# Storing a kernel's result in two DMAs, one batch row each, from two issuers

## The chip, the cores and the metric

The kernel runs on one core of one Trainium2 chip. The metric is device time in microseconds (us). The probes below were run once each, and the record marks their state unknown, so they are compared by their traces and not by their times. One run of each kernel was profiled, and its trace gives starts and durations to the nanosecond.

## The reference

One decode step (one token) for a batch of two: an adaptive layer norm, attention over the last 1024 positions of a cache with 32 heads, a second adaptive layer norm and a gated feed-forward layer.

```python
def reference(A_x, A_k_cache, A_v_cache, A_wq, A_wo, B_x, B_w_gate, B_w_up, B_w_down, c, w_mod):
    ...                                   # mod = silu(c) @ w_mod gives sa, ca, ga, sb, cb, gb
    h = _layernorm(x, axis=-1) * (1 + ca) + sa
    x = x + ga * _A_ref(h, A_k_cache, A_v_cache, A_wq, A_wo)
    h = _layernorm(x, axis=-1) * (1 + cb) + sb
    x = x + gb * _B_ref(h, B_w_gate, B_w_up, B_w_down)
    return x                              # (2, 1, 640) bfloat16: 2.5 KB
```

## The kernel before

The kernel streams caches and weights and computes as they come. Only its end matters here. The result stands in `finb`, 128 partitions by 160 columns. Eight of the rows are real: partition 32*i + 16*b holds columns 160*i to 160*i+159 of batch row b (i from 0 to 3, b 0 or 1). One DMA, issued by SyncE, stores all eight rows of 320 bytes, and SyncE waits for it as its last act. `S.dma` records a DMA with the semaphore that it is told to raise by 16; `S.op` records an operation of an engine; both work out the waits from the names read and written.

```python
        def k_dma(dst, src):                                   # L266: the line of every DMA
            return lambda e: e.dma_start(dst, src)
        ...
        S.op("dve", lambda e: e.tensor_tensor(out=fin[:, :], in0=ps[:, BK_OT, CY:CY + DR], in1=modR[:, 5, :], op=ALU.mult),
             reads=[bank(BK_OT), ("modR", 1)], writes=["fin"], name="gb_y")                   # L689
        S.op("dve", lambda e: e.tensor_tensor(out=finb[:, :], in0=fin[:, :], in1=X[:, :], op=ALU.add),
             reads=["fin", "X"], writes=["finb"], name="outR")                                # L691
        S.dma("sp", k_dma(out[:, 0, :].rearrange("b (i n) -> i b n", i=NR), finb[0:P:RB, :]),  # RB = 16
              sem_out, reads=["finb"], name="st_out")

        S.resolve()
        S.emit("sp", nc.sync, tail=lambda e: e.wait_ge(sem_out, 16))                          # L697
```

Of the kernel before, what the change touches and what calls it, by code (L numbers as in the profile page):

```python
# [119 lines left out]
def bass_adaLN_cond__sliding_block_cached__geglu_ffn__decode_kernel(  # L120
# [14 lines left out]
    P = 128  # L135
    B, _, D = A_x.shape
# [6 lines left out]
    NR = 4  # L143
# [31 lines left out]
    RB = 16  # L175
# [11 lines left out]
    with es:  # L187
        S = _Sched(nc, es)
# [54 lines left out]
        finb = sb("finb", [P, DR], BF16)  # L243
# [9 lines left out]
        def bank(k):  # L253
            return ("bank", k)
# [5 lines left out]
        sem_wu = [S.sem("d_wu%d" % i) for i in range(len(WU_SPLIT))]  # L260
        sem_wd = [S.sem("d_wd%d" % i) for i in range(len(WD_SPLIT))]
        sem_ring = [S.sem("d_ring%d" % i) for i in range(NS)]
        sem_out = S.sem("d_out")

        def k_dma(dst, src):
            return lambda e: e.dma_start(dst, src)  # L266
# [57 lines left out]
        for nm, t in (("scT", scT), ("oT", oT), ("aT", aT)):  # L324
# [6 lines left out]
             reads=["ones_f"], writes=["ident_f"], name="ident_f")  # L331
        S.op("pool", lambda e: e.tensor_copy(out=ident_b[:, :], in_=ident_f[:, :]),
             reads=["ident_f"], writes=["ident_b"], name="ident_b")
# [3 lines left out]
             reads=["ones_b"], writes=["selrow"], name="selrow")  # L337
# [3 lines left out]
             reads=["ones_b"], writes=["selg"], name="selg")  # L341
        for b in range(B):
# [4 lines left out]
                 reads=["ones_b"], writes=[("selq", b)], name="selq%d" % b)  # L347
# [4 lines left out]
             reads=["ones_b"], writes=["ztmp"], name="ztmp")  # L352
# [6 lines left out]
             reads=["ones_f", "bcL"], writes=["bcL"], name="bcLh")  # L359
# [5 lines left out]
             reads=["bcR"], writes=["bcR"] + [("bcR", z) for z in range(2)], name="bcRd")  # L365
# [4 lines left out]
             reads=["ident_f"], writes=["mask_h"], name="mask_h")  # L370
        S.op("dve", lambda e: e.tensor_reduce(out=st32[:, :], in_=ident_f[:, :].rearrange("p (i m) -> p m i", m=32), axis=AX.X, op=ALU.add),
             reads=["ident_f"], writes=["st32"], name="st32")
# [3 lines left out]
             reads=["st32"], writes=["selstat"], name="selstat")  # L376
# [3 lines left out]
        def c_T(e):  # L380
            last = None
            for j in range(KT):
# [4 lines left out]
             reads=[bank(BK_T)], writes=["scT"], name="silu")  # L387
        S.op("dve", lambda e: e.tensor_copy(out=X[:, :], in_=xr[:, :]),
             reads=["xr"], writes=["X"], name="x_f32")
# [20 lines left out]
        def ln_mod(tag, opc_idx, s_idx, dst_bf):  # L410
# [7 lines left out]
            def f(e):  # L418
# [14 lines left out]
             reads=["mask_h"], writes=["maskc"], name="maskc")  # L433
        S.op("dve", lambda e: e.tensor_reduce(out=zsel[:, :, X0:X0 + P].rearrange("p q (h m) -> p q h m", m=32)[:, :, :, 0],
                                              in_=ztmp[:, :, :, :].rearrange("p i q h -> p q h i"), axis=AX.X, op=ALU.max),
             reads=["ztmp", "zsel"], writes=["zsel"], name="zsel")

        mod_pe = []
        for half in range(2):
            def f(e, half=half):  # L440
                last = None
                for k in range(KT):
# [9 lines left out]
                 reads=[bank(half)], writes=[("modR", half)], name="mod%d_evac" % half)  # L452
            S.op("dve", lambda e, half=half: e.tensor_scalar(out=opc[:, half, :], in0=modR[:, 3 * half + 1, :], scalar1=1.0, scalar2=None, op0=ALU.add),
                 reads=[("modR", half)], writes=[("opc", half)], name="opc%d" % half)
# [17 lines left out]
        for n in range(NQB):  # L472
            if n % 2 == 0:
                S.op("act", lambda e, n=n: e.activation(out=qrow[:, n * QW:(n + 1) * QW], in_=ps[:, n, :], func=ACTF.Copy),  # L474
                     reads=[bank(n)], writes=[("qrow", n)], name="q1_evac%d" % n)
            else:
                S.op("dve", lambda e, n=n: e.tensor_copy(out=qrow[:, n * QW:(n + 1) * QW], in_=ps[:, n, :]),  # L477
                     reads=[bank(n)], writes=[("qrow", n)], name="q1_evac%d" % n)
        for u, (n, b) in enumerate((n, b) for n in range(NQB) for b in range(B)):
            bk = BK_T + u % 4  # L480
            S.op("pe", lambda e, n=n, b=b, bk=bk: e.matmul(ps[:, bk, :], lhsT=selq[:, b, :], rhs=qrow[:, n * QW:(n + 1) * QW], start=True, stop=True),
                 reads=[("selq", b), ("qrow", n)], writes=[bank(bk)], name="q2_%d_%d" % (n, b))
            S.op("act", lambda e, n=n, b=b, bk=bk: e.activation(out=qbc[:, b, n * QW:(n + 1) * QW], in_=ps[:, bk, :], func=ACTF.Copy),  # L483
                 reads=[bank(bk)], writes=[("qbc", b, n)], name="q2_evac%d_%d" % (n, b))
# [98 lines left out]
        for g in range(NG + 2):  # L583
# [23 lines left out]
            if prev:  # L607
# [5 lines left out]
             reads=[bank(BK_OT)], writes=["oT"], name="oT")  # L613
# [22 lines left out]
        for ci, (r0, nr) in enumerate(WD_SPLIT):  # L636
# [5 lines left out]
             reads=[bank(BK_M), ("modR", 0)], writes=["lnt"], name="ga_attn")  # L642
        S.op("dve", lambda e: e.tensor_tensor(out=X[:, :], in0=lnt[:, :], in1=X[:, :], op=ALU.add),
             reads=["lnt", "X"], writes=["X"], name="x1")
# [3 lines left out]
        def ffn_gu(bk, wv, name, splits):  # L648
            for ci, (k0, nk, key) in enumerate(splits):
# [12 lines left out]
             reads=[bank(0)], writes=["gl"], name="gelu")  # L662
        ffn_gu(1, wu_v, "up", [(k0, nk, ("wu", ci)) for ci, (k0, nk) in enumerate(WU_SPLIT)])
        S.op("dve", lambda e: e.tensor_tensor(out=aR[:, :], in0=ps[:, 1, 0:FT], in1=gl[:, :], op=ALU.mult),
             reads=[bank(1), "gl"], writes=["aR"], name="geglu")

        def a_T(e):
            last = None
            for i in range(NR):
# [7 lines left out]
             reads=[bank(2)], writes=["aT"], name="aT")  # L677
        for ci, (r0, nr) in enumerate(WD_SPLIT):
            def f(e, r0=r0, nr=nr):
# [10 lines left out]
             reads=[bank(BK_OT), ("modR", 1)], writes=["fin"], name="gb_y")  # L690
        S.op("dve", lambda e: e.tensor_tensor(out=finb[:, :], in0=fin[:, :], in1=X[:, :], op=ALU.add),  # L691
             reads=["fin", "X"], writes=["finb"], name="outR")
        S.dma("sp", k_dma(out[:, 0, :].rearrange("b (i n) -> i b n", i=NR), finb[0:P:RB, :]),
              sem_out, reads=["finb"], name="st_out")

        S.resolve()
        S.emit("sp", nc.sync, tail=lambda e: e.wait_ge(sem_out, 16))  # L697
        S.emit("pool", nc.gpsimd)
        S.emit("act", nc.scalar)
        S.emit("dve", nc.vector)  # L700
# [29 lines left out]
```

## Time and profile before

| | before |
|---|---|
| time, median of the three runs before the prediction | 188.83 us (188.71 to 189.14) |
| span of the profiled run | 187.6 us |
| read from HBM | 76.88 MB, 410 GB/s over the span |
| last VectorE operation (`outR`) starts | 185.52 us |
| store: issue starts, lasts | 185.87 us, 0.69 us |
| SyncE's wait for the store after that | 1.0 us |

The page of the kernel before tells what bounds it. In the DMA row each digit is the busy share of the DMA engines in one fortieth of the span, in tenths.

```profile
DMA  7999998999999999999999999999999999999991
...
HBM read 76.88 MB, written 0.00 MB: 410 GB/s over the span
## 4 chain that ended last, share of the span: by engine, by line
DMA 71%; DVE 15%; PE 7%; ACT 2%; SPq 2%; issue 1%
```

The DMA row stands at 9 in 37 of the 40 slices, and DMA is 71% of the chain of waits. The end of that chain, in order of time (start, duration, what), shows where the stream stops and the tail begins:

```profile
152.72 31.64 DMA r<-in_B_w_down_dram
184.37 0.04 issue
184.41 0.72 PE ps L684 x16
185.13 0.02 issue
185.16 0.34 DVE fin L689
185.49 0.02 issue
185.52 0.32 DVE finb L691
```

From 184.37 us on, each step waits for the one before it (it starts at most 0.04 us after that one's end), and nothing else runs. The chain stops at the last compute instruction. The timeline of the same kernel (start, duration, engine, line, operation) has the store. SPq and ACTq stand for the instruction queues of SyncE and ScalarE; the duration of a DMA on them is that of its issue, not of the transfer.

```profile
185.52 0.32 DVE L691 TENSOR_TENSOR finb<-fin,X 128x160 bf16<-128x160 f32 x1
185.87 0.69 SPq L266 DMA_DIRECT2D out_dram<-finb  x1
```

The landing is not a line of the timeline. SyncE's own waits (total us, times, longest us) show it, as the wait of line 697:

```profile
SPq L697 <- DMA out_dram<-finb: 1.0, 1, 1.0
```

So the store takes 0.69 us to issue and a further 1.0 us to land, all on the critical path. The table by stretches shows when its data moves. Its columns are the stretch, its length, busy time by engine, granted clock, DMA share and GB/s.

```profile
185.87:187.15 1.28, 0.00 (x0) 0.00 (x0) 0.00 (x0) 0.00 (x0) 0.00 (x0) 0.50 0.00 0
187.15:187.35 0.20, 0.00 (x0) 0.00 (x0) 0.00 (x0) 0.00 (x0) 0.00 (x0) 0.50 0.07 13
187.35:187.60 0.25, 0.00 (x0) 0.00 (x0) 0.00 (x0) 0.00 (x0) 0.00 (x0) 0.50 0.00 0
```

For 1.28 us after the issue's start no packet moves at all; then all of them go within 0.2 us; then comes about a quarter of a microsecond of waiting until the store has landed.

### The profile page before, as it was taken

The page shows a single profiled execution, that of the slowest core. Times are in us where ns is not written, and L with a number is a line of the kernel's source. Part 1 is how long each engine was busy: PE and PEld are TensorE (multiplying, and loading weights), DVE is VectorE, ACT ScalarE, POOL GpSimd, SP SyncE. Part 2 cuts the span into 40 slices and gives each one's busy share as a digit, 9 for nine tenths or more (in the row PEclk, how much of TensorE's full clock was granted, in tenths as well). Part 3 has the DMA queues.
Part 4 walks back from the last instruction along what each step waited for, and adds up shares of the span by engine and source line. Part 5 has one row for each costly group of instructions (what it writes and reads, how often), then busy time and mean ns, then how long its engine had stood idle before and what let it go on. Part 6 is the DMA issues. An engine that isn't in the chain of part 4 may idle for free.

```text
span 187.6 us, 2409 instructions
## 1 busy us (share of the span) xinstructions
PE 107.5 (57%) x1039; PEld 51.1 (27%) x1039; DVE 98.2 (52%) x147; ACT 29.9 (16%) x72; POOL 5.1 (3%) x23
## 2 busy tenths in 40 slices
PE   0014730742968887676676655675497395364462
PEld 0011200210323443333423323233253152353121
DVE  6131100019588988886595695775865933003211
ACT  3041100082001221112011110210120103103400
POOL 8200000000000000000000000000000000000000
PEclk9999999997587999999879999999969967569696
DMA  7999998999999999999999999999999999999991
GB/s 254 402 451 435 430 459 372 422 435 424 430 422 422 427 425 426 427 424 420 419 432 432 422 423 422 421 438 422 424 423 422 419 488 428 416 384 442 398 396 45
DMA packets 6518, 77.03 MB, mean 411 GB/s; under 512 B 746, under 2 KB 876, under 8 KB 1516
## 3 DMA queue, kind: packets, MB, share of 16 engines
q1 hardware_dynamic: 6492, 76.88, 97.1%
q8 instruction: 8, 0.13, 0.3%
q10 hardware_dynamic: 16, 0.01, 0.0%
q14 instruction: 2, 0.02, 0.0%
HBM read 76.88 MB, written 0.00 MB: 410 GB/s over the span
## 4 chain that ended last, share of the span: by engine, by line
DMA 71%; DVE 15%; PE 7%; ACT 2%; SPq 2%; issue 1%
DMA ring<-in_A_k_cache_dram 37%; DMA ring<-in_A_wq_dram 17%; DMA r<-in_B_w_down_dram 17%; DVE prod L490 9%; PE ps L502 4%; DVE S_sb L509 4%; PE ps L467 2%; SPq L266 2%; ACT qbc L483 2%; DVE ps L485 1%; DVE M L512 1%; ACT qrow L474 1%; PE ps L526 0%; DVE bcR L519 0%; PE ps L684 0%
## 5 line engine op out<-in xcount | busy, mean ns | idle before, releaser
L490 DVE TENSOR_TENSOR prod<-ring,qbc 128x3072 bf16<-128x3072 bf16 x32 | 55.9, 1751 | 14.3 <-DMA ring<-in_A_k_cache_dram 14.3
L502 PE MATMUL ps<-prod,ident_b 128*128 128x512 bf16 x192 | 52.9, 419 | 14.4 <-DVE prod L490 14.4
L502 PEld LDWEIGHTS ps<-prod,ident_b 128*128 128x128 bf16 x192 | 17.5, 104 | 40.2 <-DVE prod L490 17.5
L509 DVE TENSOR_REDUCE S_sb<-ps 128x32 f32<-128x1024 f32 x16 | 19.3, 1206 | 2.1 <-PE ps L502 2.1
L526 PE MATMUL ps<-bcR,bcL 5*128 5x4 f32 x32 | 6.1, 258 | 21.9 <-DVE bcR L519 21.9
L563 ACT ACTIVATE On<-ps,rden 128x384 bf16<-128x384 f32 x16 | 9.3, 580 | 43.5 <-DVE rden L561 21.1
L551 PE MATMUL ps<-ring,E_sb 128*8 128x384 bf16 x256 | 15.5, 369 | 0.0
L534 ACT ACTIVATE E_sb<-Sb_sb 128x128 bf16<-128x128 f32 x16 | 5.0, 310 | 56.4 <-DVE Sb_sb L531 56.4
L467 PE MATMUL ps<-ring,hT 128*2 128x512 bf16 x60 | 6.7, 626 | 9.8 <-DMA ring<-in_A_wq_dram 8.8
L526 PEld LDWEIGHTS ps<-bcR,bcL 5*128 5x128 f32 x32 | 4.7, 183 | 26.1 <-DVE bcR L519 26.1
L477 DVE CAST qrow<-ps 128x512 bf16<-128x512 f32 x1 | 0.7, 692 | 15.7 <-PE ps L467 15.7
L622 PE MATMUL ps<-ring,oT 128*17 128x160 bf16 x192 | 5.5, 294 | 5.6 <-DMA ring<-in_A_wo_dram 5.6
L531 DVE TENSOR_TENSOR Sb_sb<-S_sb,ps 128x128 f32<-128x128 f32 x16 | 4.6, 287 | 7.6 <-PE ps L526 7.6
L540 PEld LDWEIGHTS ps<-denp,maskc 128*128 128x128 f32 x32 | 7.1, 224 | 3.7 <-ACT E_sb L534 0.9
L641 DVE TENSOR_TENSOR lnt<-ps,modR 128x160 f32<-128x160 f32 x1 | 0.3, 325 | 12.6 <-PE ps L622 12.6
L445 PE MATMUL ps<-r,scT 128*17 128x480 bf16 x40 | 4.3, 597 | 3.9 <-DMA r<-in_w_mod_dram 3.9
L622 PEld LDWEIGHTS ps<-ring,oT 128*17 128x17 bf16 x192 | 4.9, 117 | 6.2 <-DMA ring<-in_A_wo_dram 6.2
L551 PEld LDWEIGHTS ps<-ring,E_sb 128*8 128x8 bf16 x256 | 5.1, 90 | 3.7 <-issue 1.2
L396 PE MATMUL ps<-st,selstat 128*128 128x2 f32 x4 | 0.9, 298 | 8.6 <-ACT sqj L392 8.6
L467 PEld LDWEIGHTS ps<-ring,hT 128*2 128x2 bf16 x60 | 1.7, 114 | 14.7 <-DMA ring<-in_A_wq_dram 9.7
L576 PE MATMUL ps<-On,zsel 128*128 128x96 bf16 x64 | 5.2, 241 | 0.7 <-ACT On L563 0.7
L540 PE MATMUL ps<-denp,maskc 128*128 128x1 f32 x32 | 5.1, 230 | 0.8 <-ACT E_sb L534 0.8
(81 smaller groups left out, 71.2 us busy)
## 6 DMA issues: line engine op xcount, KB each, us to landing
ring<-in_A_k_cache_dram SPq DMA_DIRECT2D x16, 1536.0 KB, 24.4
ring<-in_A_v_cache_dram SPq DMA_DIRECT2D x16, 1536.0 KB, 24.2
r<-in_w_mod_dram SPq DMA_DIRECT2D x1, 4800.0 KB, 14.3
ring<-in_A_wq_dram SPq DMA_DIRECT2D x1, 4608.0 KB, 32.3
ring<-in_A_wo_dram SPq DMA_DIRECT2D x1, 4480.0 KB, 23.4
ring<-in_A_wq_dram SPq DMA_DIRECT2D x1, 3072.0 KB, 21.2
ring<-in_A_wo_dram SPq DMA_DIRECT2D x1, 2720.0 KB, 24.1
r<-in_B_w_gate_dram SPq DMA_DIRECT2D x1, 1920.0 KB, 25.0
```

The costliest lines, as they stand in the source:

```text
L467: last = e.matmul(ps[32 * i:32 * i + B, n, :], lhsT=hT[:, k, :], rhs=wv[:, kk, i, n * QW:(n + 1) * QW], start=(k == 0), stop=(k == KT - 1) ...
L490: S.op("dve", lambda e: e.tensor_tensor(out=prod[:, 2 * (g % 2) + ci, :, :], in0=ring[:, sl, ci * JC * Dh:(ci + 1) * JC * Dh].rearrange("p ...
L502: last = e.matmul(o_ap, lhsT=ident_b[:, :], rhs=prod[:, pz, :, t * GC:(t + 1) * GC], start=(t == 0), stop=(t == NCH - 1))
L509: S.op("dve", lambda e: e.tensor_reduce(out=S_sb[:, z, :], in_=ps[:, 2 * z:2 * z + 2, :].rearrange("p k (j c) -> p (k j) c", c=GC), axis=A ...
L526: S.op("pe", lambda e: e.matmul(ps[:, BK_T, P:P + HQ], lhsT=bcL[:, :], rhs=bcR[:, z, :], start=True, stop=True), reads=[("bcR", z), "bcL"] ...
L531: S.op("dve", lambda e: e.tensor_tensor(out=Sb_sb[:, z, :, :], in0=S_sb[:, z, :].unsqueeze(2).broadcast_to([P, J, HQ]), in1=ps[:, BK_T, P: ...
L534: S.op("act", lambda e: e.activation(out=E_sb[:, z, :, :], in_=Sb_sb[:, z, :, :], func=ACTF.Exp, scale=SCALE, accum_out=denp[:, z:z + 1]), ...
L540: S.op("pe", lambda e: e.matmul(ps[:, BK_T, P + 16:P + 17], lhsT=maskc[:, :], rhs=denp[:, z:z + 1], start=True, stop=True), reads=[("denp" ...
L551: last = e.matmul(ps[32 * i:32 * i + 2 * HQ, BK_O, 0:ON], lhsT=E_sb[:, z, 2 * jp:2 * jp + 2, :].rearrange("p j h -> p (j h)"), rhs=ring[:, ...
L563: S.op("act", lambda e: e.activation(out=On[:, quad % 2, b, :], in_=ps[:, BK_O, 0:ON], func=ACTF.Identity, scale=rden[:, z:z + 1]), reads= ...
L576: last = e.matmul(ps[:, BK_OT, 0:B * NT].rearrange("p (b t) -> p b t", b=B), lhsT=zsel[:, jj, x:x + P], rhs=On[:, quad % 2, :, jj * Dh + d ...
L622: last = e.matmul(ps[32 * i:32 * i + RM, BK_M, 0:DR], lhsT=oT[:, t, :], rhs=wv[:, tl, i, :], start=(t == 0), stop=(t == NT - 1), tile_posi ...
```

## The change

The intent: two smaller stores, issued at the same moment by two engines, should each be issued and landed sooner than one. ScalarE has been idle since its GELU ended at 177.94 us.

```diff
-        sem_out = S.sem("d_out")
+        sem_out = [S.sem("d_out%d" % b) for b in range(B)]
...
-        S.dma("sp", k_dma(out[:, 0, :].rearrange("b (i n) -> i b n", i=NR), finb[0:P:RB, :]),
-              sem_out, reads=["finb"], name="st_out")
+        for b, eng in enumerate(("sp", "act")):
+            S.dma(eng, k_dma(out[b, 0, :].rearrange("(i n) -> i n", i=NR), finb[RB * b:P:32, :]),
+                  sem_out[b], reads=["finb"], name="st_out%d" % b)

         S.resolve()
-        S.emit("sp", nc.sync, tail=lambda e: e.wait_ge(sem_out, 16))
+        S.emit("sp", nc.sync, tail=lambda e: [e.wait_ge(s, 16) for s in sem_out])
```

## The prediction

> **What bounds the kernel now.** It streams weights and caches: the profile page counts 76.88 MB read from HBM, and its DMA row stands at 9 in almost all of the 40 slices. The chain of waits gives DMA 71% of the span; its last DMA piece, the load of B_w_down, ends at 184.37 us. Behind it comes a serial tail in which no load moves (the table by stretches shows a DMA share of 0.00 from 184.40 to 185.85 us): matmuls 0.72 us, two VectorE operations (0.33 and 0.32 us), then the store. The timeline shows its issue on SyncE from 185.87, lasting 0.69 us; the queue's own waits show 1.0 us until it lands; the span ends at 187.6.
>
> **What the change does.** It touches only those last 1.7 us. The rows of TensorE, VectorE and GpSimd are unchanged; the SyncE store shrinks from 4x2x160 to 4x160, and ScalarE gets one more row at its very end. ScalarE's last operation, the GELU, ends at 177.94 us, so it is free some 8 us before the result is ready. Bytes are the same (2.5 KB, now 1.25 KB twice) and so are the runs of 320 bytes (8 in all). One more semaphore is waited on.
>
> Costs from the trace:
> - Issue. It hardly follows size: large SyncE loads take 0.33 to 0.54 us undisturbed, ScalarE's two small loads 0.56 (2 rows) and 0.64 us (8 rows), the store 0.69. I estimate 0.55 to 0.65 us for a 4-row half: a gain of 0.05 to 0.15 us if the two issues do not disturb each other.
> - They may. [...] In this trace SyncE's second load of A_wq took 0.70 us where the first took 0.41, while ScalarE issued the load of A_x (1.41 to 2.05 us): an estimate of up to 0.3 us of delay for one half.
> - Landing. 1.0 us for 2.5 KB is latency, not bytes; I expect the same for each half. [...]
> - The second wait on SyncE: 17 ns, as the one there is.
>
> All of it is on the critical path, and the end is the later half. Sum: -0.15 to +0.3 us, +0.05 in the middle, 0.03% of the time. The three runs before spread over 0.43 us.
>
> **Predicted time: 188.85 us, 188.4 to 189.3 (8 in 10). Faster by over 2%: 0.5%; within 2%: 99%; slower by over 2%: 0.5%.** To be 2% faster the change would have to save 3.8 us, more than twice the whole stretch from the store's issue to the end.
>
> **What would show it.** Right: all up to the last VectorE operation is as before; two issues start within 0.05 us of each other; each lasts 0.55 to 0.7 us, or one is longer by up to 0.3 us [...]; the last landing comes about 1.0 us after the later issue; the span stays within 0.3 us of 187.6. Wrong: a landing well under 1.0 us (then bytes or rows per DMA matter), or a ScalarE issue that starts late.
>
> **What would make it wrong.** A slow issue or completion on ScalarE's queue, idle since the start; a shift of the load stream larger than the change; another granted clock (0.90 mean, 0.60 in the tail's matmuls).

The sum: its low end, -0.15 us, is the larger gain in issue; its high end, +0.3 us, is the delay estimated from the issues of the two A_wq loads (0.70 us against 0.41).

## The result, and the profile after

| | before | after |
|---|---|---|
| median of five runs each | 188.94 us (188.71 to 189.14) | 189.12 us (188.97 to 189.41) |
| ratio | | 1.0013 (95%: 1.0001 to 1.0026) |
| span of the profiled run | 187.6 us | 188.0 us |
| from the store's issue to its last landing | 1.715 us | 1.998 us |

A ratio is the mean time of one kernel's runs over the mean of the other's from the same rounds, so it is not quite the ratio of the medians. Here the means are 189.17 and 188.92 us: 0.25 us apart. By the measure of 2% the time is the same.

First the timeline of the kernel after:

```profile
185.65 0.33 DVE L691 TENSOR_TENSOR finb<-fin,X 128x160 bf16<-128x160 f32 x1
186.00 0.66 SPq L266 DMA_DIRECT2D out_dram<-finb  x1
186.00 0.57 ACTq L266 DMA_DIRECT2D out_dram<-finb  x1
```

The last addition starts 0.13 us later than before. That lies upstream of the change: over the twelve traces, every kernel included, it starts anywhere from 185.41 to 185.98 us. The span of one trace is therefore no measure of an effect of 0.3 us; the time from the store's issue to its landing is. The two issues start together, and each is shorter than the single one was. Yet SyncE's waits show a longer landing:

```profile
SPq L698 <- DMA out_dram<-finb: 1.3, 1, 1.3
```

and the table by stretches of the kernel after shows why:

```profile
186.00:187.22 1.22, 0.00 (x0) 0.00 (x0) 0.00 (x0) 0.00 (x0) 0.00 (x0) 0.50 0.00 0
187.22:187.35 0.13, 0.00 (x0) 0.00 (x0) 0.00 (x0) 0.00 (x0) 0.00 (x0) 0.50 0.06 10
187.35:187.57 0.22, 0.00 (x0) 0.00 (x0) 0.00 (x0) 0.00 (x0) 0.00 (x0) 0.50 0.00 0
187.57:187.70 0.13, 0.00 (x0) 0.00 (x0) 0.00 (x0) 0.00 (x0) 0.00 (x0) 0.50 0.06 10
187.70:188.02 0.32, 0.00 (x0) 0.00 (x0) 0.00 (x0) 0.00 (x0) 0.00 (x0) 0.50 0.00 0
```

There are now two bursts of packets, with 0.22 us between them in which no packet moves. The trace's single records of packets and semaphores, which these views add up, say whose they are. All times are in us from the start of the span:

```
before   SyncE half+half : issue 185.868   early record 186.937   packets from 187.152   landings 187.535 .547 .558 .583
after    ScalarE half    : issue 186.002   early record 187.005   packets from 187.230   landings 187.579 .592 .613 .637
after    SyncE half      : issue 185.998   early record 187.362   packets from 187.579   landings 187.937 .948 .960 .996
```

Each of these stores leaves five records on its semaphore: an early one before any packet, and four landings. What the early record stands for the trace does not say. In these three the first packet follows it by about 0.22 us, in the late store as in the others (187.579 - 187.362 = 0.217), so the early record is taken here to tell when a store really got going.

SyncE's half got going 0.357 us after ScalarE's, though its issue began 4 ns sooner and its recorded issue is over 0.707 us before (186.655). The last landing comes at 187.996, 0.36 us after that of ScalarE's half. The question is what holds it. (That ScalarE's goes first fits a later run, scalar_half_early: undisturbed, a half makes its early record 1.006 us after its issue on ScalarE and 1.031 us on SyncE.)

### The profile page after: what moved, and what is told of

It reads as the page before. It is cut to its first block, busy times and chain, and to the rows that moved or that the text cites. A ratio compares the mean times of both kernels' runs of the same rounds, so it can differ in the third digit from the quotient of the medians.

```text
span 188.0 us, 2409 instructions
## 1 busy us (share of the span) xinstructions
PE 104.0 (55%) x1038; PEld 50.3 (27%) x1039; DVE 98.1 (52%) x147; ACT 29.9 (16%) x72; POOL 5.1 (3%) x23
## 4 chain that ended last, share of the span: by engine, by line
DMA 71%; DVE 16%; PE 6%; ACT 2%; SPq 2%; issue 1%
DMA ring<-in_A_k_cache_dram 37%; DMA ring<-in_A_wq_dram 17%; DMA r<-in_B_w_down_dram 17%; DVE prod L490 10%; DVE S_sb L509 4%; PE ps L502 3%; PE ps L467 2%; SPq L266 2%; ACT qbc L483 2%; DVE ps L485 1%; DVE M L512 1%; ACT qrow L474 1%; PE ps L526 0%; DVE bcR L519 0%; PE ps L684 0%
## 5 line engine op out<-in xcount | busy, mean ns | idle before, releaser
L502 PE MATMUL ps<-prod,ident_b 128*128 128x512 bf16 x192 | 50.7, 406 | 14.9 <-DVE prod L490 14.9
L551 PE MATMUL ps<-ring,E_sb 128*8 128x384 bf16 x256 | 14.5, 351 | 0.0
L467 PE MATMUL ps<-ring,hT 128*2 128x512 bf16 x60 | 6.2, 586 | 10.1 <-DMA ring<-in_A_wq_dram 9.1
L622 PE MATMUL ps<-ring,oT 128*17 128x160 bf16 x192 | 6.3, 321 | 7.5 <-DMA ring<-in_A_wo_dram 7.5
L622 PEld LDWEIGHTS ps<-ring,oT 128*17 128x17 bf16 x192 | 5.7, 129 | 7.9 <-DMA ring<-in_A_wo_dram 7.9
L540 PEld LDWEIGHTS ps<-denp,maskc 128*128 128x128 f32 x32 | 6.6, 208 | 3.5 <-ACT E_sb L534 0.9
L576 PE MATMUL ps<-On,zsel 128*128 128x96 bf16 x64 | 4.3, 214 | 0.7 <-ACT On L563 0.7
```

Source lines behind the costliest of these rows:

```text
L467: last = e.matmul(ps[32 * i:32 * i + B, n, :], lhsT=hT[:, k, :], rhs=wv[:, kk, i, n * QW:(n + 1) * QW], start=(k == 0), stop=(k == KT - 1) ...
L502: last = e.matmul(o_ap, lhsT=ident_b[:, :], rhs=prod[:, pz, :, t * GC:(t + 1) * GC], start=(t == 0), stop=(t == NCH - 1))
L540: S.op("pe", lambda e: e.matmul(ps[:, BK_T, P + 16:P + 17], lhsT=maskc[:, :], rhs=denp[:, z:z + 1], start=True, stop=True), reads=[("denp" ...
L551: last = e.matmul(ps[32 * i:32 * i + 2 * HQ, BK_O, 0:ON], lhsT=E_sb[:, z, 2 * jp:2 * jp + 2, :].rearrange("p j h -> p (j h)"), rhs=ring[:, ...
L622: last = e.matmul(ps[32 * i:32 * i + RM, BK_M, 0:DR], lhsT=oT[:, t, :], rhs=wv[:, tl, i, :], start=(t == 0), stop=(t == NT - 1), tile_posi ...
```

## The experiments

Three theories stood at the start.

- **Turns.** Something that SyncE and ScalarE have in common, which no trace shows, serves them in turn; the second store waits for the first.
- **Shared engines.** Both halves go through the same DMA engines, and a packet of the second waits there for a packet of the first to land. This too was an assumption: the records used here do not say which engine moved a packet. The records above fit it strikingly: SyncE's packets start at 187.579, 187.592, 187.607 and 187.639, and ScalarE's half lands at 187.579, 187.592, 187.613 and 187.637.
- **The split itself.** ScalarE's queue, unused since the start, or the second semaphore and wait cost the time.

Except for after_again and single_on_scalar (five runs each), every experiment is one run and one trace. This table has, for every run, the times of each store in us from the start of its own issue, read from the trace's records.

| run | store | issue lasts | early record | first packet | last landing |
|---|---|---|---|---|---|
| before | SyncE, 8 rows | 0.691 | 1.069 | 1.284 | 1.715 |
| after | ScalarE, 4 rows | 0.575 | 1.003 | 1.228 | 1.635 |
| after | SyncE, 4 rows | 0.657 | **1.364** | 1.581 | **1.998** |
| after_again | ScalarE, 4 rows | 0.575 | 1.003 | 1.226 | 1.638 |
| after_again | SyncE, 4 rows | 0.657 | **1.365** | 1.580 | **1.991** |
| scalar_half_early | SyncE, 4 rows, alone | 0.653 | 1.031 | 1.247 | 1.662 |
| single_on_scalar | ScalarE, 8 rows, alone | 0.608 | 1.030 | 1.246 | 1.682 |
| both_on_sync | first 4 rows | 0.652 | 1.030 | 1.249 | 1.657 |
| both_on_sync | second 4 rows (issued 0.700 later) | 0.563 | 0.974 | 1.198 | 1.606 |
| sync_half_later | ScalarE, 4 rows | 0.576 | 1.003 | 1.229 | 1.640 |
| sync_half_later | SyncE, 4 rows (issued 0.229 later) | 0.653 | 1.142 | 1.357 | 1.769 |
| half_on_gpsimd | SyncE, 4 rows | 0.656 | 1.035 | 1.256 | 1.656 |
| half_on_gpsimd | GpSimd, 4 rows (issued 0.268 later) | 0.707 | none | 1.277 | 1.745 |
| probe_1row | ScalarE, 1 row to scratch | 0.241 | 0.410 | 0.715 | 1.076 |
| probe_1row | SyncE, 8 rows | 0.692 | 1.069 | 1.286 | 1.722 |
| probe_2rows | ScalarE, 2 rows to scratch | 0.612 | 1.040 | 1.257 | 1.625 |
| probe_2rows | SyncE, 8 rows | 0.694 | **1.402** | 1.622 | **2.046** |
| probe_4rows_big | ScalarE, 4 rows of 12 KB | 0.535 | 0.961 | 1.181 | 2.497 |
| probe_4rows_big | SyncE, 8 rows | 0.695 | **1.324** | 2.040 | 2.686 |
| probe_128rows | ScalarE, 128 rows to scratch | 0.366 | none | 0.854 | 1.529 |
| probe_128rows | SyncE, 8 rows | 0.691 | 1.069 | 1.285 | 1.722 |

### after_again: is it there every time?

The edit: none.

> The changed kernel once more, for the size and for the order of the two halves. If the 0.3 us in its trace is systematic: one half lands about 1.63 us and the other about 2.0 us after the issues' start, the ratio lies between 1.0005 and 1.0025, and the median is 0.1 to 0.4 us above that of before. If it was chance: both halves land within 0.1 us of each other and the ratio's interval spans 1.0.

Measured: median 189.23 us (189.02 to 189.59) against 188.86 (nine runs, 188.73 to 189.31), ratio 1.0010 (95%: 0.9996 to 1.0024). By itself this interval does not exclude 1.0. The trace does show the same delay to within a few nanoseconds: early records 0.357 us apart, last landing 1.991 us after the first issue. The hold is systematic; its effect on the whole time is just about as large as the scatter of runs.

### scalar_half_early: does the split itself cost?

```diff
+        S.dma("act", k_dma(out[1, 0, :].rearrange("(i n) -> i n", i=NR), hrow[RB:P:32, :]),
+              sem_out[1], reads=["hrow"], name="st_out1")
         ffn_gu(1, wu_v, "up", ...)
...
-        for b, eng in enumerate(("sp", "act")):
-            ...
+        S.dma("sp", k_dma(out[0, 0, :].rearrange("(i n) -> i n", i=NR), finb[0:P:32, :]),
+              sem_out[0], reads=["finb"], name="st_out0")
```

> Wrong on purpose: ScalarE stores stale rows (of hrow) to out[1] right after the GELU, about 8 us before the end; SyncE stores its true half at the end, and both semaphores are still waited on. Measure: time from the start of SyncE's store issue to the last landing of its semaphore; before 1.72 us, changed kernel 2.00 us. If the two issues at the same moment are the cause [...], the SyncE half alone should take 1.65 to 1.75 us, and the span about 187.6. If the split itself costs (second semaphore, second wait, a half being slower), it stays near 2.0 us.

Measured: the result is wrong; 188.84 us, one run. ScalarE's store was issued at 177.96 us. SyncE's half, now alone in time, landed 1.662 us after its issue's start. Everything that the split adds is still there (two queues, two semaphores, two waits), and the delay is gone (timeline, and SyncE's wait):

```profile
185.91 0.65 SPq L266 DMA_DIRECT2D out_dram<-finb  x1
SPq L699 <- DMA out_dram<-finb: 1.0, 1, 1.0
```

The third theory falls. The experiment also prices a half: 0.053 us less than the whole (1.662 against 1.715), most of it in the issue (0.653 against 0.691).

### single_on_scalar: is ScalarE slow?

```diff
-        S.dma("sp", k_dma(out[:, 0, :].rearrange("b (i n) -> i b n", i=NR), finb[0:P:RB, :]),
+        S.dma("act", k_dma(out[:, 0, :].rearrange("b (i n) -> i b n", i=NR), finb[0:P:RB, :]),
```

> The whole store (8 rows, as before) issued by ScalarE alone. If ScalarE's queue, idle for long, were the slow part, the time from issue start to last landing would be over the 1.72 us of before, by up to 0.3 us. In the changed kernel ScalarE's half was served first and landed 1.63 us after its issue start, so I expect 1.63 to 1.72 us and a ratio of 0.9990 to 1.0005.

Measured: 1.682 us from issue to last landing, within the expected range, and median 188.99 us against 188.96, ratio 1.0000 (95%: 0.9986 to 1.0014). ScalarE's queue, idle until then, was no slower. In this one trace its issue is 0.083 us shorter than SyncE's and the landing 0.033 us sooner; the timed runs show no gain from it.

### both_on_sync: the split without a second issuer

```diff
-        for b, eng in enumerate(("sp", "act")):
+        for b, eng in enumerate(("sp", "sp")):
```

> Both halves issued by SyncE, one after the other. The second issue starts when the first ends, 0.6 to 0.66 us later. [...] its packets start a full issue time after the first's: last landing about 2.3 us after the first issue's start (span about 188.2). If packets have to wait for completion of the first on the same engine, that wait (0.4 us after the first's start) is over by then as well: the same 2.3 us. So it gives the price of the split without a second issuer, against 2.00 us with one; under 2.0 us would refute both.

Measured: 189.46 us, one run; last landing 2.306 us after the first issue's start, as expected. A second store on the same queue comes 0.65 us behind (packets from 187.116 and from 187.765). With two issuers the second comes only 0.36 us behind (1.998 us in all). So the second issuer does save time against this version; it does not save enough to beat not splitting. It saves 0.31 of the 0.65 us that one issuer puts between them, rounded (2.306 against 1.998 us in all).

### probe_1row: a first try at turns against engines

```diff
+        sem_scr = S.sem("d_scr")
+        scr = nc.dram_tensor("scr", (1, DR), BF16, kind="Internal").ap()
...
+        S.dma("act", k_dma(scr[:, :], finb[0:1, :]),
+              sem_scr, reads=["finb"], name="st_scr")
```

SyncE's store is the one of before, and SyncE waits for both semaphores.

> SyncE's store as in the kernel before (8 rows), plus a store of one row by ScalarE to a scratch tensor at the same moment. [...] whichever store is served second is delayed as a whole; if it is SyncE's, all four [...] start together, some 0.2 to 0.35 us later than the 1.28 us after issue start of before, and its early [...] is late by the same time. Shared engines (a packet waits for the completion of the other store on its own engine): only one of [...] SyncE's store starts late, by about 0.35 us; the other three start at about 1.28 us[...].

The parts that are cut assumed how a store is split up and what its early record means; of the counts that are left, the records show the four, as the four landings of SyncE's store; the others are assumptions. In terms of the records the two outcomes were: if the stores take turns, the second one is late as a whole, from its early record on; if packets wait for landings, its early record is on time and only some of its packets are late, by about 0.35 us.

Measured: 188.90 us, one run; SyncE's store was not delayed at all (1.069, 1.286 and 1.722 us). Both theories can live with that, since the one-row store is out of the way too soon. Its early record comes 0.410 us after its issue and SyncE's 0.655 us later, so even a turn as long as the 0.357 us of the changed kernel would have been over before SyncE's store came to it. The expectation had overlooked this when it said that the store served second is delayed in any case. Whether a one-row store holds another at all, this probe can't tell. The one-row store is far quicker than the others: packet at 0.715 us, landing at 1.076 us, where the 8-row store takes 1.284 and 1.715.

### probe_2rows: the experiment that decides

The edit is that of the one-row probe with `(2, DR)` and `finb[0:17:16, :]`.

> As the one-row probe, with two rows [...] stored by ScalarE to a scratch tensor beside SyncE's unchanged store of 8 rows. The one-row store took only 0.24 us to issue and was out of the way, so it told nothing of a conflict. [...] if ScalarE's is served first [...] SyncE's store start late by the same 0.1 to 0.35 us, and the early [...] (1.07 us after issue start undisturbed) is late by as much. Shared engines: two [...] start late by about 0.35 us, two on time (1.28 us), [...].

The first outcome is that of turns. In terms of the records the two were, as in the one-row probe: early record and packets late together by 0.1 to 0.35 us, or the early record on time (1.07 us) and part of the packets late.

Measured: 189.19 us, one run. SyncE's early record came at 1.402 us instead of 1.069, and its packets started from 1.622 us on instead of 1.284. The timeline and SyncE's waits of this run:

```profile
185.87 0.69 SPq L268 DMA_DIRECT2D out_dram<-finb  x1
185.88 0.61 ACTq L268 DMA_DIRECT2D scr<-finb  x1
```

```profile
SPq L701 <- DMA out_dram<-finb: 1.4, 1, 1.4
```

The 1.4 us here against 1.0 us before is the delay of the unchanged 8-row store, with an issue as long as before (0.69). ScalarE's two rows left two landings, SyncE's eight rows four. The records:

```
probe_2rows  ScalarE 2 rows : early record 186.918   packets from 187.135   landings 187.493 .503
probe_2rows  SyncE   8 rows : early record 187.275   packets from 187.495   landings 187.869 .881 .893 .919
```

SyncE's early record, late by 0.333 us, comes at 187.275, 0.218 us before ScalarE's first landing, so it did not wait for a landing. The first packet follows it by 0.220 us, against 0.215 us before, so no further wait shows between the two. And all four landings keep the spacing of before (12, 12 and 26 ns here, 12, 11 and 25 ns there): the store is late as a whole. The shared-engine theory falls; the close fit of its times in the changed kernel was a coincidence. The gap between the two early records is 0.357 us, the same for two rows as for four.

### probe_4rows_big: does the hold grow with the bytes?

The edit is that of the one-row probe with `(4, SLOT)` and `ring[0:P:32, 0, :]`, four rows of 12 KB.

> ScalarE stores four rows of 12 KB ([...] 38 times the bytes) to a scratch tensor beside SyncE's unchanged store of 8 rows. [...] about 0.35 us late (at 1.43 us after its issue start instead of 1.07), no later than in the changed kernel, in spite of the larger data[...]

The expectation is about SyncE's early record under the first theory.

Measured: 189.72 us, one run. The early records are 0.358 us apart (186.728 and 187.086), with 38 times the bytes. Counted from SyncE's own issue its early record came at 1.324 us; I had expected 1.43, because I had not foreseen that ScalarE's own would come sooner too (0.961). SyncE's packets came much later, from 2.040 us after the issue on, 0.716 us after the early record instead of 0.215; those of the large rows took 0.82 to 0.94 us each. They may have waited for the large ones, which the records do not show. It is another thing than the hold: the early records stay 0.358 us apart.

### half_on_gpsimd: another issuer

```diff
-        for b, eng in enumerate(("sp", "act")):
+        for b, eng in enumerate(("sp", "pool")):
```

> The second half issued by GpSimd in place of ScalarE. [...] SyncE's half lands undisturbed, 1.65 to 1.72 us after its issue start[...]. If anything issued at the same moment delays SyncE's half, it lands near 2.0 us.

The expectation rested on an assumption about how GpSimd issues a DMA; no run here shows it. Measured: 189.46 us, one run. SyncE's half was not delayed (1.656 us). GpSimd's issue started 0.268 us later than SyncE's and its half landed 1.745 us after that, 2.013 us after SyncE's issue began. For SyncE's half this is the expected outcome, but weak evidence: starting later, GpSimd's store could have come second in any queue. As a version it ends no sooner than the split over SyncE and ScalarE.

### sync_half_later: a delay that should cost nothing

```diff
+        S.op("dve", lambda e: e.tensor_tensor(out=lnt[:, :], in0=fin[:, :], in1=X[:, :], op=ALU.add),
+             reads=["fin", "X"], writes=["lnt", "stag"], name="stagger")
...
-                  sem_out[b], reads=["finb"], name="st_out%d" % b)
+                  sem_out[b], reads=["finb"] + (["stag"] if eng == "sp" else []), name="st_out%d" % b)
```

> The changed kernel with SyncE's half held back: it also waits for one more VectorE addition of 128x160 (about 0.36 us with its gap), ScalarE's half does not. [...] a fixed hold of 0.357 us per store: the two issues are now spaced by about that hold, so SyncE's half is not delayed after its own issue ([...] last landing at about 1.66 us after it), and counted from the start of ScalarE's issue the last landing comes at 2.0 to 2.05 us, as in the changed kernel: 0.36 us of delay that costs nothing. If the 0.357 us is paid at any rate by the second store, the last landing comes at about 2.36 us.

Measured: 189.21 us, one run. The extra operation overlapped with the one before it, so the issues were 0.229 us apart, not 0.36. SyncE's half was delayed by 0.11 us after its own issue (early record 1.142 against 1.031 alone), and the early records were 0.368 us apart. The last landing came 1.998 us after ScalarE's issue, as in the changed kernel. Holding one half back by 0.23 us cost nothing, which is what a turn of fixed length gives, and what a fixed penalty on the second store does not: with that, the delay would have stayed at 0.33 us and the last landing would have come at about 2.22 us (an estimate: 0.229 + 1.662 + 0.333). The timeline and SyncE's wait of this run:

```profile
185.86 0.58 ACTq L266 DMA_DIRECT2D out_dram<-finb  x1
186.09 0.65 SPq L266 DMA_DIRECT2D out_dram<-finb  x1
SPq L700 <- DMA out_dram<-finb: 1.1, 1, 1.1
```

No run held ScalarE's half back instead, so the order of the two was never reversed.

### probe_128rows: how far it goes

The edit is that of the one-row probe with `(P, DR)` and `finb[:, :]`, 128 rows of 320 bytes.

> ScalarE stores 128 rows of 320 bytes [...] to a scratch tensor beside SyncE's unchanged store of 8 rows. [...] If the hold is fixed per store, SyncE's store is again late by 0.25 to 0.36 us (its packets start at 1.53 to 1.64 us after its issue). If the hold grows with the rows, much later. If a [...] store takes a shorter way (issues of 128-row loads took 0.33 to 0.54 us), like the one-row store, SyncE's packets start undelayed at about 1.28 us.

Measured: 189.02 us, one run. SyncE's store was not delayed (1.069, 1.285, 1.722). ScalarE's store left sixteen landings and no early record; its issue took 0.366 us and its last landing came at 1.529 us, sooner than that of the 8-row store with a sixteenth of the bytes. Of the three outcomes named, it is the last. That does not show that a store of 128 rows takes no turn. It got going early, as the one-row store did: its first packet came at 0.854 us, and a packet follows its store's start by 0.22 us (four or eight rows) to 0.31 us (one row), so it got going some 0.43 to 0.52 us before SyncE's store (an estimate from these numbers). All the runs together fit one reading: stores that would have got going at nearly the same moment came out 0.357 to 0.368 us apart, and stores that were further apart anyway (0.644 us in both_on_sync, 0.655 us in probe_1row, and this one) were not held. The two early stores are also the ones with short issues (0.241 and 0.366 us against 0.535 to 0.612 for ScalarE's other stores). A probe that brings such a store to the same moment was not run.

### No version that was built beats the kernel before

The experiments show two quicker kinds of store, of one row (1.076 us) and of 128 rows (1.529 us). The result's eight rows are neither: they stand on partitions 16 apart, in a memory order of four by two, and every store here of all or half of them that was not held took 1.61 to 1.75 us. Other ways, such as eight stores of one row, were not built. Issuing the single store from ScalarE showed no gain. So the kernel before stands.

## Why the prediction was right, and which term was off

The time, 189.12 us, lies within 188.4 to 189.3, and the change is within 2%. The argument was that the change can touch only the last 1.7 us, and the traces bear that out. The range is 0.9 us wide and the effect 0.28, so that the time fell inside says little about the mechanism; the traces have to tell. Point by point:

- **The bound.** Right. The load stream ends at 184.37 us before and 184.47 after, and what follows is serial.
- **The gain in issue, "0.05 to 0.15 us".** A little too high. The issue of SyncE's half, alone, is 0.038 us shorter (0.653 against 0.691), and it lands 0.053 us sooner (scalar_half_early). Splitting the bytes saves almost nothing, since most of the time passes before the first packet (1.247 of the 1.662 us).
- **The delay of one half, "an estimate of up to 0.3 us".** That one half is held behind the other was right; its size and its weight were off, and its place too (below): this is the mis-sized term. It is 0.333 us on the early record (1.364 against 1.031), above the upper end, and it is there every time, while the middle of the sum, "+0.05", took it as an occasional part. The sum is now 0.333 - 0.053 = +0.28 us, as the traces have it (1.998 - 1.715 = 0.283); the timed means show +0.25.
- **The evidence for it.** Weak. I read the 0.70 us issue of the second load of A_wq as a sign that one issuer holds the other up. In the trace after, ScalarE issues the load of A_x at the same place (1.40 us, 0.66 long), and that SyncE issue takes 0.43 us. But then the next SyncE issue, the first load of k_cache, is longer (first the kernel before, then after):

```profile
1.70 0.70 SPq L266 DMA_DIRECT2D ring<-in_A_wq_dram  x1
2.44 0.63 SPq L266 DMA_DIRECT2D ring<-in_A_k_cache_dram  x1
```

```profile
1.70 0.43 SPq L266 DMA_DIRECT2D ring<-in_A_wq_dram  x1
2.17 0.76 SPq L266 DMA_DIRECT2D ring<-in_A_k_cache_dram  x1
```

  All twelve traces fall in these two kinds: A_wq 0.63 to 0.70 us and k_cache 0.63 to 0.64 in three, A_wq 0.42 to 0.43 and k_cache 0.74 to 0.85 in nine. So something may lengthen a SyncE issue there, now one and now the other; no run takes ScalarE's load away, so the cause stays open. The hold of the stores does not lengthen the recorded issue at all (next point). That the estimate was near was in part luck.
- **"One of them is longer by up to 0.3 us".** Wrong in place. Both recorded issues keep their length (SyncE's 0.657 us, against 0.653 alone). The delay lies after the recorded issue, in what the waits call landing.
- **"The last landing comes about 1.0 us after the later issue".** Wrong: 1.34 us after the end of SyncE's issue (187.996 - 186.655), against 1.06 us for ScalarE's half.
- **"The span stays within 0.3 us of 187.6".** It was 188.0. Of the 0.4, 0.13 us was there before the store.
- **The second wait, and a slow ScalarE queue.** The wait costs nothing that shows, and the queue is not slow (scalar_half_early, single_on_scalar).

What is shown: two stores, of two to eight rows, issued at one moment from SyncE and ScalarE, get going 0.357 or 0.358 us apart in all four traces that have such a pair, with 0.6 to 48 KB in ScalarE's store, and the delay is there in the early record, before the held store moves its first packet. That something in common serves them in turn is the reading that fits this and sync_half_later (0.368 us apart, with issues 0.229 us apart). What that is, no run shows. Whether stores of one row and of 128 rows take such a turn too stays open: in the two probes they got going too early to meet the other store.

## What to carry to other kernels

The store at the end of this kernel is latency and not bytes: 1.7 us for 2.5 KB, of which the packets take 0.1. Issued from SyncE or ScalarE with nothing in its way, a store here took from issue to last landing 1.08 us for one row, 1.62 for two rows, 1.61 to 1.72 for four or eight, and 1.53 for 128 rows (40 KB). Splitting it over two issuers shortened nothing that matters here and made one half wait its turn, so in this kernel it stays one DMA. The delay came before the packets (probe_2rows: early record late by 0.333 us), and after the recorded issue, which is as long for the held half as for a free one (0.657 against 0.653 us). When an effect is smaller than the scatter of whole runs, measure the stretch that the change touches in the trace, and compare it with the same stretch where the suspected partner has been moved away in time.
